# Gated scan and top-1 mixture of experts: the first 192 steps go through both frequent experts in place of being sorted by expert

## The chip, the cores and the metric

The kernel runs on one core of a Trainium2 chip. The metric is the device time of one execution in microseconds (us). An engine takes its instructions in the order in which the program lists them; the engines are PE (TensorE, matrix products), DVE (VectorE), ACT (ScalarE), POOL (GpSimd) and SP (SyncE, which here only starts transfers). They wait for each other by semaphores.

## The reference, cut to what matters

Four sequences of 5056 steps and 256 channels run through a gated linear recurrence. Each of the 20224 resulting tokens then goes to one of eight experts, a two-layer network, and is multiplied by the probability of that expert.

```python
batch, seq, d_model = (4, 5056, 256)
N, D, E, F = (20224, 256, 8, 1024)
...
for t in range(S):
    h = a_t[:, t] * h + x_gated[:, t]
    y[:, t] = h
...
logits = x @ w_gate + modality_bias[modality_id]
e_idx = np.argmax(logits, axis=1)
...
for e in range(E):
    mask = e_idx == e
    h = np.maximum(x[mask] @ w1[e], 0.0)
    out[mask] = gate_w[mask, None] * (h @ w2[e])
```

There are two modalities, and the bias of each (spread 0.5) is large against the rest of the logits. The reference's own router on its default inputs gives 10051 tokens to expert 4, 10124 to expert 7, 49 to expert 2 and none to the others. Of the 768 tokens in the first 192 steps of the four sequences it gives 389 to expert 4, 377 to expert 7 and 2 to expert 2.

## The kernel before, in words

**Chunks.** The sequences are cut along time into the chunks of `CHUNKS` (first step, steps): two of 128 steps, eighteen of 256, one of 128 and one of 64. A chunk holds four times as many tokens as steps. For each chunk ACT and DVE compute the gates and run the scan (`scan_chunk`; on DVE the wide operations on tiles `g` and `x`, and the scan over `a`, `g`), scale and split the result into two fp16 halves in place of `a` (`split_chunk`; `mxy`, `miy`, `scy` and `ivy` belong to its scale), PE computes the logits into `psl`, and DVE finds each token's expert, its place among that expert's tokens, and its gate (`route_chunk`; `l`, `ky`, `oh`, `cu`, `dt`, `be`, `di`, `sg`). `be` counts, for each expert, the rows given out so far. `rows_part` transposes the tokens (SP, tile `rt`) and POOL scatters each as a row to its expert's stretch of the buffer `rows` in device memory.

**Pages.** The experts work on pages of 256 or 128 rows that are read back from `rows` (SP: tile `X` transposed, and `mt` with the token's number and gate). The `HOT` = 2 experts of largest bias, here 4 and 7, have their weights converted to fp16 halves once, in `hw`; `wr` holds them as they come from memory, in four buffers. `choose_two` takes one page for each of the two experts (here called a round): `u` is how far an expert's pages have got, `sel` the rows at which the two pages begin, which SP reads. While the program is built, `choose_pages` adds rounds as long as the tokens of the chunks routed so far, less a margin (`behind`), cover them. The numbers of rounds and pages are thus fixed in the program, while which rows a page holds is decided on the chip. Before the change that gives one round of 128 rows, 38 rounds of 256, then a last round of 256 and one of 128, whose pages take what is left of their expert; and one page of 128 (`choose_cold`) for the expert with most tokens outside the two, whose weights are loaded and converted for it (`cold_weights`, raw tiles `cr`, converted `cw`).

**Layers.** A page's first layer (`ph`, 48 products) is followed by ACT and DVE, which write its result as two fp16 halves `H`; the second layer (`po`) follows, ACT multiplies by the gate (`ot`), and POOL scatters the 128 rows to the output. The first layer of a page is interleaved with the second layer of the page before it.

**What is left over.** When the fixed pages are through, the program compares what has been given out with what the pages took (`over`, `left_over`). If a row is left, `more_pages` runs two more pages of 128, each with the weights of its expert loaded and converted anew, then looks again, and so on. Each engine has a branch of its own there (L1157).

**Order.** The instructions of all engines are written out by a planner that runs while the program is built: the generators ask for an engine and an assumed duration, and of those that could begin at about the same time the one of lowest priority number goes next. `START` gives the order of the first loads: chunk 0, the first expert's two matrices, chunk 1, the second expert's, chunk 2. `HI` says which engine writes the upper fp16 halves of each weight matrix (A is ACT, D is DVE).

Of the kernel before, what the change touches and what calls it, by code (L numbers as in the profile page):

```python
# [9 lines left out]
F32 = mybir.dt.float32  # L10
# [23 lines left out]
HOT = 2  # L34
WAIT = 3.0
WINDOW = 0.1
PART = 8
BACKLOG = 9000
LOOK = 384
HI = "ADADAD"  # L40
LO = "DDDDDD"
START = "0 w w 1 w w 2"
W_AT = 9
C_STEP = 2
URGENT = 0.1
ROW_STEP = 2.4
LAG = 3.0
W_STEP = 0.1

# [6 lines left out]
def columns(c):  # L56

    return B * CHUNKS[c][1] // P


# [14 lines left out]
def kernel(  # L75
# [80 lines left out]

    u = const.tile([1, HOT], F32, name="u")
    nc.vector.tensor_scalar(out=u, in0=key[:, 0:HOT, 0], scalar1=NCAP / 256.0, scalar2=None, op0=ALU.mult)
    cold = const.tile([1, E], F32, name="cold")
    nc.vector.tensor_scalar(out=cold, in0=ev, scalar1=HOT - 0.5, scalar2=8.0, op0=ALU.is_ge, op1=ALU.mult)  # L160
# [269 lines left out]
    def load_chunk(c):  # L430

        t0, T = CHUNKS[c]
        cols = 2 * B * T
        base = 2 * B * t0
        z = T / 256
        got = []
        if f"{c}" in loads:
            yield "SP", 0.0, seen(("turn", loads.index(f"{c}") - 1)), 0.0
        else:
            yield "SP", 0.0, allof(drained(sum(B * t for _, t in CHUNKS[: c + 1]) - BACKLOG), seen(("load", c - 1))), -3.0  # L440
        for i, (name, src) in enumerate((("a", rs), ("g", gs), ("x", xs))):
            tag = "H" if c == 0 and name != "g" else name
            yield "DMA", 2.9 * z, room(tag), -9.0
            tickets[c, name] = tag, take(tag)
            t = (pm if tag == "H" else pa).tile([P, cols], F32, name=f"{name}{c}", tag=tag, bufs=BUFS[tag])
# [95 lines left out]
    wg16 = const.tile([P, 2, 2 * E], F16, name="wg16")  # L541
    ivg = const.tile([P, 1, 1], F32, name="ivg")

    def gate_weights():
# [6 lines left out]
        ps = psl.tile([P, 512], F32, name="psg", tag="lg")  # L551
        yield from power_of_two("g", mx[:, 0:1], 1, ps, sc[:, 0:1], ivg)
        give("lg", tl)
        yield "DVE", 0.07, None
# [21 lines left out]
    def split_chunk(c):  # L576
# [4 lines left out]
        z = T / 256  # L581
        lag = LAG if c > 6 else 0.2
        yield "DVE", 0.07 + 2.13 * z, allof(seen(("scan", c)), room("lg"), seen("gate"), *([seen(("sized", c - 1))] if c else [])), lag
# [36 lines left out]
        for k in range(C):  # L620
            if k % 2 == 0:
                yield "PE", 0.2, None, 1.25 if c > 6 else 0.0
            mm = [(s, h) for s in range(2) for h in range(2)]
# [6 lines left out]
        y_free(c)  # L630

    def y_free(c):
        if ("lg", c) in mark and all(("tr", c, j) in mark for j in range(parts(c))):
            done(c, "a")

    def rows_part(c, j):
# [17 lines left out]
        y_free(c)  # L654

        if T < P:
            for u in range(2):
                nc.gpsimd.iota(
                    rt[64 * u : 64 * u + 64, 0:k, D], pattern=[[2 * S, k]], base=t0 + S * u, channel_multiplier=1
                )  # L660
        else:
            nw = T // P
            nc.gpsimd.iota(
                rt[:, 0:k, D].rearrange("p (q w) -> p q w", w=nw), pattern=[[S, k // nw], [P, nw]],
                base=t0 + S * (PART * j // nw), channel_multiplier=1,
            )
        yield "DVE", 0.07, seen(("route", c)), 0.0
# [4 lines left out]
        for u in range(k):  # L672
            yield "POOL", ROW_STEP if c > 6 else 1.3, None
            scatter(f"rows{c}", rt[:, u, 0:ROW], di[:, PART * j + u : PART * j + u + 1])
# [3 lines left out]
    def route_chunk(c):  # L678
        C = columns(c)
        order = [("route", c - 1)] if c else []  # L680
        lag = LAG if c > 6 else 0.2
        yield "DVE", 0.2, seen(("lg", c), *order)
# [28 lines left out]
        oh = sm.tile([P, E, C], F16, name=f"oh{c}", tag="oh")  # L711
        nc.vector.tensor_tensor(out=oh, in0=ky, in1=mx.broadcast_to(sh), op=ALU.is_equal)
        yield "DVE", 0.13, None
        cu = sm.tile([P, E, C], F16, name=f"cu{c}", tag="cu")
# [40 lines left out]
        di = sm.tile([P, C], I32, name=f"di{c}", tag="di", bufs=6)  # L755
        nc.vector.tensor_copy(di, df)
        tiles["route", c] = di, sg
# [4 lines left out]
    def scatter(group, src, idx):  # L762
# [12 lines left out]
        if "pe" in count:  # L775
# [3 lines left out]
            )  # L779

    nt = const.tile([P, ROW], I32, name="nt")
# [3 lines left out]
    nc.gpsimd.tensor_copy(nf, pidx.broadcast_to([P, E]))  # L785

    def null_rows():
# [18 lines left out]
    class Page:  # L806
        pass

    pages, queue = [], []
    count = {"chosen": 0, "ended": False, "cold": 0, "rows": 0}  # L810
# [9 lines left out]
    def enough():  # L820
# [17 lines left out]
    def queue_page(pg):  # L838
        pg.n = len(pages)
        pages.append(pg)  # L840
        if pg.n == 0:
            add(load_rows(), (1, 2), plan["end"])
            add(expert_layers(), (5, 0), plan["end"])

# [126 lines left out]

    class Tile:
        pass

    def load_rows(n=0):
        while True:
# [5 lines left out]
            if True:  # L982
# [4 lines left out]
                t = Tile()  # L987
                t.tx = take("X")
                t.pg, t.n = pg, f"{pg.n}"
# [21 lines left out]
    def layer1_tail(t, f2, ph, tp):  # L1011
# [11 lines left out]
        mark["h", t.n, f2] = plan["end"]  # L1023

    def layer2_tail(t, a, po, tp):
# [4 lines left out]
        free["DMA"] = max(free["DMA"], plan["end"] - 1.04) + 0.37  # L1030
        ins = nc.gpsimd.indirect_dma_start(  # L1031
            out=out[:, :], out_offset=bass.IndirectOffsetOnAxis(ap=t.mt[:, a, 0:1], axis=0),
            in_=t.ot[:, a, :], in_offset=None, bounds_check=N - 1, oob_is_err=False,
        ).ins
        tc.declare_no_dep(ins, group="outs", reason="every token has an output row of its own")
        tc.add_to_no_dep_group("outs", ins)
        if a == t.pg.st // P - 1:
            give("ot", t.to)

    def ready_at(t):  # L1040
        return max(t.ready, mark.get(("cw", t.pg.c), FAR) if t.pg.e is None else mark.get(("w", 2 * t.pg.e), FAR))

    def expert_layers():

        prev = None
        while True:
# [7 lines left out]
            for g in range(4):  # L1054
                if cur is not None:
# [5 lines left out]
                    if g == 0:  # L1061
                        cur.th = take("H")
                        used.append((plan["end"], st + (used[-1][1] if used else 0)))
                        cur.H = pm.tile([P, 2, NF, st], F16, name=f"H{cur.n}", tag="H")
# [13 lines left out]
                    if g == 3:  # L1078
                        if cur.tx is not None:
                            give("X", cur.tx)  # L1080
                        if pg.e is None:
                            give("wr", pg.tw[0])
                if prev is not None:
# [9 lines left out]
                    if g == 0:  # L1093
                        conds.append(room("ot"))
                        if pg.e is not None:
                            conds.append(seen(("hot", pg.e)))
                    yield "PE", 1.312 * z, allof(*conds), 0.0
                    if g == 0:
                        prev.to = take("ot")
                        prev.ot = pm.tile([P, na, D], F32, name=f"ot{prev.n}", tag="ot", bufs=3)  # L1100
                        gates = prev.mt[:, :, 1].bitcast(F32)
                        prev.gt = sm.tile([P, na], F32, name=f"gt{prev.n}", tag="gt", bufs=3)
# [18 lines left out]
                    if f == NF - 1:  # L1121
                        add(layer2_tail(prev, a, po, prev.tp), (0, 1), plan["end"] + 0.2)
                    if g == 3:
# [4 lines left out]

    def start_chunk(c):
        add(load_chunk(c), (0, 10 + C_STEP * c))  # L1130
        add(scan_chunk(c), (0, 11 + C_STEP * c), urgent=c == 0)
        add(split_chunk(c), (0, 10 + C_STEP * c), urgent=c == 0)
        add(route_chunk(c), (0, 9 + C_STEP * c), urgent=c == 0)
        for j in range(parts(c)):
# [5 lines left out]
    for m in range(2 * HOT):  # L1140
        add(hot_weights(m), (2, W_AT + W_STEP * m))
    add(choose_pages(), (0, 4), urgent=True)
# [75 lines left out]
```

## Time and profile before

| | us |
|---|---|
| median of 3 runs (lowest, highest) | 986.11 (985.5, 986.31) |
| the profiled execution, by the device | 987.44 |
| its span, first to last instruction | 985.6 |
| PE busy in the span | 894.6 |
| DVE, ACT, POOL busy | 667.6, 568.4, 471.3 |

The profile has a page of totals, and answers to queries of its trace. A row of the timeline gives the start in us, the duration, the engine, the line of the kernel, the operation, what it writes and reads with partitions x elements, how many instructions the row merges, and in brackets how long the engine had been idle and who ended that. A row of groups gives a line's instructions of one shape with their count, then busy us and mean ns of one. A window's row gives for each engine the busy us and the number of instructions, then the granted clock of TensorE (PEclk, 1.00 is full), the share of the transfer engines and GB/s.

### The profile page before, as it was taken

Reading aid. Unit: us, or ns where it says so; the run is one execution under the profiler, and the core shown is the slowest. Engines: PE = TensorE matmul, PEld = TensorE weight load, DVE = VectorE, ACT = ScalarE, POOL = GpSimd, SP = SyncE. Lnnn points to the kernel's source line nnn. Section 1 sums busy time; section 2 is a strip of 40 time slices with the busy share of each in tenths; the row PEclk is TensorE's granted clock in tenths of the full one; section 3 lists DMA queues with packets and bytes.
Section 4 is the critical chain, followed back from the end, with each engine's and each line's share of the span. In section 5 each row is a group of like instructions: output and inputs, shape, how many; then the busy total and the mean of one; then the engine's idle time right before and its main releaser. Section 6 shows DMA issues by size and latency. Waiting matters only on the chain. (4 is left out here: it accounts for less than half of the span.)

```text
span 985.6 us, 22594 instructions
## 1 busy us (share of the span) xinstructions
PE 894.6 (91%) x8700; PEld 791.9 (80%) x8700; DVE 667.6 (68%) x1531; ACT 568.4 (58%) x790; POOL 471.3 (48%) x501
## 2 busy tenths in 40 slices
PE   2224899999999999999999999999999999999997
PEld 1223787888888888888888888888898988888886
DVE  4989888888998879997788998952353332232321
ACT  6757776878875687758588787533333333333332
POOL 4034655746386673876746675554253111111111
PEclk9997999999999999999999999999999999999999
DMA  8548997877879897699897887554452222222210
GB/s 296 212 144 219 233 215 233 271 156 188 225 161 232 220 251 222 130 208 197 267 247 171 202 176 171 130 116 102 118 130 71 57 50 53 51 50 55 50 39 19
DMA packets 221176, 156.13 MB, mean 158 GB/s; under 512 B 197953, under 2 KB 201154, under 8 KB 214146
## 3 DMA queue, kind: packets, MB, share of 16 engines
q1 hardware_dynamic: 204178, 110.43, 47.6%
q0 software_dynamic: 16176, 43.98, 13.7%
q8 instruction: 70, 1.15, 0.5%
q14 instruction: 48, 0.39, 0.1%
q10 hardware_dynamic: 704, 0.18, 0.1%
HBM read 68.76 MB, written 44.35 MB: 115 GB/s over the span
## 5 line engine op out<-in xcount | busy, mean ns | idle before, releaser
L1075 PE MATMUL ph<-X,hw 128*128 128x256 f16 (+1 forms) x3936 | 476.4, 272 | 2.6 <-DMA X<-rows 2.6
L1117 PE MATMUL po<-hw,H 128*128 128x256 f16 x3840 | 473.1, 273 | 5.9 <-DVE H L1018 5.9
L1117 PEld LDWEIGHTS <-H 128*128 128x128 f16 x3864 | 372.9, 98 | 51.9 <-DVE H L1018 6.7
L1075 PEld LDWEIGHTS <-hw 128*128 128x128 f16 x3936 | 376.7, 99 | 46.9 <-issue 3.0
L1018 DVE SCALAR_TENSOR_TENSOR H<-ph,H 128x512 f16<-128x512 f32 (+1 forms) x332 | 219.9, 669 | 250.5 <-ACT H L1016 247.1
L1031 POOL DMA_INDIRECT out_dram<-ot,mt x161 | 205.9, 1279 | 297.9 <-ACT ot L1027 239.2
L1016 ACT ACTIVATE H<-ph 128x512 f16<-128x512 f32 (+1 forms) x332 | 191.5, 580 | 269.0 <-PE ph L1075 264.6
L763 POOL DMA_INDIRECT rows<-rt,di x158 | 206.4, 1306 | 184.8 <-PE ph L1075 55.6
L1027 ACT ACTIVATE ot<-po,gt 128x256 f32<-128x256 f32 x161 | 76.0, 472 | 87.7 <-PE po L1117 66.5
L497 DVE TENSOR_TENSOR_SCAN g<-a,g 128x2048 f32<-128x2048 f32 (+2 forms) x22 | 87.8, 3990 | 0.8
L607 ACT ACTIVATE a<-g,scy 128x512 f16<-128x512 f32 (+2 forms) x88 | 54.9, 670 | 7.1 <-DVE miy L520 4.9
L610 DVE SCALAR_TENSOR_TENSOR a<-g,scy,a 128x512 f16<-128x512 f32 (+2 forms) x88 | 56.9, 693 | 0.0
L483 DVE TENSOR_TENSOR g<-g,x 128x2048 f32<-128x2048 f32 (+2 forms) x22 | 45.5, 2069 | 8.6 <-ACT x L481 8.5
L474 ACT ACTIVATE a<-a,ch 128x1024 f32<-128x1024 f32 (+2 forms) x44 | 49.4, 1146 | 0.1
L477 ACT ACTIVATE x<-a 128x2048 f32<-128x2048 f32 (+2 forms) x22 | 38.1, 1733 | 17.2 <-issue 10.5
L469 DVE SCALAR_TENSOR_TENSOR g<-g,x 128x2048 f32<-128x2048 f32 (+2 forms) x22 | 45.6, 2075 | 0.4 <-ACT g L465 0.4
L586 DVE TENSOR_REDUCE mxy<-g 128x4 bf16<-128x2048 f32 (+2 forms) x22 | 45.3, 2059 | 0.2 <-issue 0.2
L625 PEld LDWEIGHTS <-a 128*128 128x128 f16 x632 | 25.5, 97 | 19.7 <-ACT a L607 10.8
L481 ACT ACTIVATE x<-x 128x2048 f32<-128x2048 f32 (+2 forms) x22 | 38.2, 1736 | 4.4 <-DVE x L479 4.2
L465 ACT ACTIVATE g<-g 128x2048 f32<-128x2048 f32 (+2 forms) x22 | 38.1, 1734 | 2.8 <-DMA g<-in_i_gate_dram 2.7
L467 ACT ACTIVATE a<-a 128x2048 f32<-128x2048 f32 (+2 forms) x22 | 38.0, 1726 | 0.0
L625 PE MATMUL psl<-wg,a 128*128 128x16 f16 x632 | 26.6, 170 | 12.1 <-DVE a L610 5.9
(174 smaller groups left out, 438.4 us busy)
## 6 DMA issues: line engine op xcount, KB each, us to landing
a<-in_r_gate_dram SPq DMA_DIRECT2D x18, 1024.0 KB
g<-in_i_gate_dram SPq DMA_DIRECT2D x18, 1024.0 KB
x<-in_x_dram SPq DMA_DIRECT2D x18, 1024.0 KB
wr<-in_moe_w_dram SPq DMA_DIRECT2D x4, 1024.0 KB
out_dram<-ot,mt POOLq DMA_INDIRECT x161
rows<-rt,di POOLq DMA_INDIRECT x158
cr<-in_moe_w_dram SPq DMA_DIRECT2D x2, 1024.0 KB
a<-in_r_gate_dram SPq DMA_DIRECT2D x3, 512.0 KB
```

The lines of the kernel that those rows point to most:

```text
L474: nc.scalar.activation(sl, sl, AF.Exp, scale=ch[:, h : h + 1], bias=ch[:, h : h + 1])
L497: nc.vector.tensor_tensor_scan(out=g, data0=a, data1=g, initial=0.0, op0=ALU.mult, op1=ALU.add)
L607: nc.scalar.activation(ys[:, 0, :, g, :], yg[:, :, g, :], AF.Copy, scale=sc[:, g : g + 1])
L610: nc.vector.scalar_tensor_tensor(out=ys[:, 1, :, g, :], in0=yg[:, :, g, :], scalar=sc[:, g : g + 1], in1=ys[:, 0, :, g, :], op0=ALU.mult, ...
L625: nc.tensor.matmul(ps[:, 2 * E * k : 2 * E * (k + 1)], yc[:, s, h, k, :], wg16[:, h, :], start=(m == 0), stop=(m == len(mm) - 1),)
L763: ins = nc.gpsimd.indirect_dma_start(out=rows[:, :], out_offset=bass.IndirectOffsetOnAxis(ap=idx, axis=0), in_=src, in_offset=None, bounds ...
L1016: nc.scalar.activation(t.H[:, 0, hs, :], ph[:, :, 0:st], AF.Relu)
L1018: nc.vector.scalar_tensor_tensor(out=t.H[:, 1, hs, :], in0=ph[:, :, 0:st], scalar=0.0, in1=t.H[:, 0, hs, :], op0=ALU.max, op1=ALU.subtract,)
L1027: nc.scalar.activation(t.ot[:, a, :], po, AF.Copy, scale=t.gt[:, a : a + 1])
L1031: ins = nc.gpsimd.indirect_dma_start(out=out[:, :], out_offset=bass.IndirectOffsetOnAxis(ap=t.mt[:, a, 0:1], axis=0), in_=t.ot[:, a, :], i ...
L1075: ins = nc.tensor.matmul(ph[:, v, 0:st], lhsT, rhs, start=(m == 0), stop=(m == len(mm) - 1))
L1117: ins = nc.tensor.matmul(po, lhsT, rhs, start=(f == 0 and m == 0), stop=(f == NF - 1 and m == len(mm) - 1))
```

## The change: what it does

The first two chunks of 128 steps become three of 64 and one of 128, and the chunks of 256 begin at step 320 and end the cut with one of 128 (`CHUNKS`). The chunks 0, 1 and 2, of 64 steps and 256 tokens each, are `DENSE`. Their tokens do not go through pages if they belong to one of the two frequent experts: PE applies each of the two experts to all 256 tokens as they lie in `a`, six tiles in the order of `DENSE_ORDER` (chunk, part, expert). `dense_tail` multiplies a tile's result by the token's gate if the token belongs to that expert and by 0 if not (`g2`, `gt`); ACT writes the first expert's part to `do`, DVE adds the second's, and POOL scatters the sum to the output. `route_chunk` makes for these chunks three rows of masks (`h3c`, `sel3`: first expert, second, any other), counts in `be` only the tokens of other experts, and gives the rest a row number outside `rows`, which the scatter skips.

In `enough` and `choose_pages` the tokens of the dense chunks now count as none (`rows_of`). The rounds in the program become one of 128, then 36 of 256, then the last one of 256 and the last of 128; 79 pages in place of 83, besides the six dense tiles. All upper halves of the two experts' weights are now written by ACT (`HI`), the weights' conversion goes ahead of the chunks (`W_AT`), and expert work is started by the dense tiles (`expert_layers` is added at the start and no longer by the first page).

```diff
-CHUNKS = [(0, 128), (128, 128)] + [(256 + 256 * k, 256) for k in range(18)] + [(4864, 128), (4992, 64)]
+CHUNKS = [(0, 64), (64, 64), (128, 64), (192, 128)] + [(320 + 256 * k, 256) for k in range(18)] + [(4928, 128)]
+DENSE = 3
-HI = "ADADAD"
+HI = "AAAAAD"
-W_AT = 9
+W_AT = [2, 2, 4, 4]
+DENSE_ORDER = [(0, 0, 0), (1, 0, 0), (0, 0, 1), (1, 0, 1), (2, 0, 0), (2, 0, 1)]
+def rows_of(c):
+    return B * CHUNKS[c][1] if c >= DENSE else 0
...
+    def dense_ready(t):
+        at = allof(seen(*[("split", t.c, j) for j in range(parts(t.c))], ("w", 2 * t.pg.e)))()
+        if at < FAR and t.c not in dense:
+            ys = tiles[t.c][0].bitcast(F16).rearrange("p (x n) -> p x n", x=4)
+            o = pm.tile([P, columns(t.c), D], F32, name=f"do{t.c}", tag=f"do{t.c}", bufs=1)
+            dense[t.c] = ys, o
+        return at
...
@@ route_chunk
+        if c < DENSE:
+            nc.vector.tensor_tensor(
+                out=h3c, in0=oh.rearrange("p (o e) c -> p o e c", o=1).broadcast_to(s4), in1=hot3.broadcast_to(s4), op=ALU.mult
+            )
+            nc.vector.tensor_reduce(out=sel3, in_=h3c.rearrange("p r e c -> p r c e"), axis=AX.X, op=ALU.add)
+            oh = h3c[:, HOT]
...
+            nc.vector.scalar_tensor_tensor(
+                out=df, in0=sel3[:, HOT], scalar=-float(NULL_ID), in1=df, op0=ALU.mult, op1=ALU.add
+            )
+            nc.vector.tensor_scalar(out=di, in0=df, scalar1=float(NULL_ID), scalar2=None, op0=ALU.add)
+            nc.vector.tensor_tensor(out=gd[:, 0], in0=tiles["iv", c][0], in1=sg, op=ALU.mult)
+            nc.vector.tensor_tensor(out=g2, in0=sel3[:, 0:HOT], in1=gd.broadcast_to([P, HOT, C]), op=ALU.mult)
+            nc.vector.scalar_tensor_tensor(
+                out=to, in0=sel3[:, HOT], scalar=float(NULL_ID), in1=tokens[c], op0=ALU.mult, op1=ALU.add
+            )
...
@@ enough, choose_pages
-            have += B * CHUNKS[c][1]
+            have += rows_of(c)
-            have = sum(B * t for _, t in CHUNKS[: routed(plan["end"])])
+            have = sum(rows_of(c) for c in range(routed(plan["end"])))
...
+    def dense_tail(t, a, po, tp):
+        _, o = dense[t.c]
+        k = 2 * t.i + a
+        if a == 0:
+            nc.vector.tensor_scalar(out=t.gt, in0=gates, scalar1=hiv[t.pg.e], scalar2=None, op0=ALU.mult)
+        if t.pg.e == 0:
+            nc.scalar.activation(o[:, k, :], po, AF.Copy, scale=t.gt[:, a : a + 1])
+            return
+        nc.vector.scalar_tensor_tensor(
+            out=o[:, k, :], in0=po, scalar=t.gt[:, a : a + 1], in1=o[:, k, :], op0=ALU.mult, op1=ALU.add
+        )
+        put_out(o[:, k, :], tiles["gates", t.c][1][:, k : k + 1])
...
+    for c, i, e in DENSE_ORDER:
+        dense_tile(c, i, e)
+    add(expert_layers(), (5, 0))
```

On DVE, before the change, the first pages are chosen (L863 to L875) behind the scan of the third chunk (L497); `psl_550` holds the second chunk's logits:

```order
L497 SCALAR_TENSOR_TENSOR g_433<-a_406,g_433 128x2048
L863 TENSOR_TENSOR d_644<-b_575,u 1x2
L685 TENSOR_REDUCE l_646<-psl_550 128x32
L865 TENSOR_SCALAR d_644<-d_644 1x2
L867 SCALAR_TENSOR_TENSOR sel_643<-u,d_644 1x2
L873 TENSOR_SCALAR d_644<-d_644 1x2
L875 TENSOR_TENSOR u<-u,d_644 1x2
```

Nothing of an expert's layers stands ahead of this choice. After the change DVE has, behind the scan of the fourth chunk, the tails of the dense tiles: `Hd` is the lower half of a dense tile's hidden layer, `do` the sum of the two experts, `g_640<-g_640,x_858` the first wide operation of the fifth chunk.

```order
L1102 SCALAR_TENSOR_TENSOR Hd_0_1_1040<-phd_0_1_0_1041,Hd_0_1_1040 128x512
L721 TENSOR_TENSOR l_1108<-l_1108,ivl_989 128x16
L482 SCALAR_TENSOR_TENSOR g_640<-g_640,x_858 128x2048
L1102 SCALAR_TENSOR_TENSOR Hd_0_1_1040<-phd_0_1_1_1095,Hd_0_1_1040 128x512
L1117 TENSOR_SCALAR gtd_0_1_1168<-g_833,hiv_219 128x2
L1124 SCALAR_TENSOR_TENSOR do_507<-pod_0_1_0_1066,gtd_0_1_1168,do_507 128x256
```

Such tails of the six dense tiles (24 of `Hd`, 6 of `do` by DVE) are new between the chunks' own work.

The first pages are now chosen further down on DVE, behind the routing of the fifth chunk (`di_1760`) and the first wide operation of the sixth:

```order
L794 TENSOR_REDUCE df_1758<-dt_1748 128x8
L818 CAST di_1760<-df_1758 128x8
L482 SCALAR_TENSOR_TENSOR g_1602<-g_1602,x_1667 128x2048
L950 TENSOR_TENSOR d_1767<-b_1643,u 1x2
L700 TENSOR_TENSOR rt_0_1717<-ivy_1506,sg_1742 128x8
L952 TENSOR_SCALAR d_1767<-d_1767 1x2
L954 SCALAR_TENSOR_TENSOR sel_1766<-u,d_1767 1x2
```

The choice has thus moved behind the work of further chunks and behind all dense tiles.

At the end of the fixed pages DVE stands before the change as follows; the branch is L1157, and the rows behind it are those of `more_pages`:

```order
L1103 TENSOR_SCALAR gt_14986<-mt_14632,hiv_216 128x1
L1018 SCALAR_TENSOR_TENSOR H_14893<-ph_3_14964,H_14893 128x256
L1157 TENSOR_LOAD over_14410
L1157 COMPARE_AND_BRANCH
L890 TENSOR_TENSOR k_15038<-be,tk 1x8
L904 SCALAR_TENSOR_TENSOR k_15038<-k_15038,tieb 1x8
```

After the change the same rows stand there under new line numbers, behind four pages fewer. On SP, which starts the transfers, the rows behind its branch (L1281 after the change) are these, `X_15388` being the first further page and `cr_0` the first of its expert's two weight matrices (`ISA` rows set registers):

```order
L1281 COMPARE_AND_BRANCH
L1069 TENSOR_LOAD sel_15347
L1069 ISA x2
L1080 ISA
L1080 DMA_TRANSPOSE X_15388<-rows 128x4x128
L1081 ISA
L1081 DMA mt_15389<-rows 128x2
L410 TENSOR_LOAD sel_15347
L410 ISA x2
L378 ISA
L378 DMA cr_0_15401<-in_moe_w_dram 128x2x1024
```

Nothing moved on this stretch but its place: it stands behind 79 pages where it stood behind 83. What a row of these lists does not tell is how long it takes or waits.

More of the change, by code (lines that the diff above doesn't have):

```diff
@@ L542 @@
     ivg = const.tile([P, 1, 1], F32, name="ivg")
+    hot3 = const.tile([P, HOT + 1, E, 1], F16, name="hot3")
     def gate_weights():
@@ L630, in split_chunk, with dense_tile @@
         y_free(c)
+    def dense_tile(c, i, e):
+        t = Tile()
+        t.pg = Page()
+        t.pg.st, t.pg.e, t.c, t.i, t.tx, t.n = 256, e, c, i, None, f"d{c}_{i}_{e}"
+        queue.append(t)
+    def dense_ready(t):
[5 more added lines that the diff above has]
+        return at
+    dense = {}
     def y_free(c):
-        if ("lg", c) in mark and all(("tr", c, j) in mark for j in range(parts(c))):
+        taken = all(("taken", *t) in mark for t in DENSE_ORDER if t[0] == c)
+        if taken and ("lg", c) in mark and all(("tr", c, j) in mark for j in range(parts(c))):
             done(c, "a")
@@ L654, in rows_part @@
         y_free(c)
[L656 to L666, printed above, removed]
+        numbers(rt[:, :, D], c, j)
         yield "DVE", 0.07, seen(("route", c)), 0.0
@@ L785 @@
     nc.gpsimd.tensor_copy(nf, pidx.broadcast_to([P, E]))
+    tokens = {}
+    for c in range(DENSE):
+        ti = const.tile([P, columns(c)], I32, name=f"ti{c}")
+        numbers(ti, c, 0)
+        tokens[c] = const.tile([P, columns(c)], F32, name=f"tn{c}")
+        nc.gpsimd.tensor_copy(tokens[c], ti)
     def null_rows():
@@ L807 @@
         pass
+    class Tile:
+        pass
     pages, queue = [], []
@@ L1023, in layer1_tail, with put_out @@
         mark["h", t.n, f2] = plan["end"]
+    def dense_tail(t, a, po, tp):
+        _, o = dense[t.c]
+        k = 2 * t.i + a
+        yield "DVE", 0.07, allof(seen(("gates", t.c)), seen(("hot", t.pg.e))), 0.0
+        if a == 0:
+            t.gt = sm.tile([P, 2], F32, name=f"gt{t.n}", tag="gt", bufs=3)
+            gates = tiles["gates", t.c][0][:, t.pg.e, k : k + 2]
+            nc.vector.tensor_scalar(out=t.gt, in0=gates, scalar1=hiv[t.pg.e], scalar2=None, op0=ALU.mult)
+        if t.pg.e == 0:
+            yield "ACT", 0.36, None
+            nc.scalar.activation(o[:, k, :], po, AF.Copy, scale=t.gt[:, a : a + 1])
+            give("po", tp)
+            return
+        yield "DVE", 0.36, None
+        nc.vector.scalar_tensor_tensor(
+            out=o[:, k, :], in0=po, scalar=t.gt[:, a : a + 1], in1=o[:, k, :], op0=ALU.mult, op1=ALU.add
+        )
+        give("po", tp)
+        yield "POOL", 1.04, None
+        put_out(o[:, k, :], tiles["gates", t.c][1][:, k : k + 1])
+    def put_out(src, idx):
+        free["DMA"] = max(free["DMA"], plan["end"] - 1.04) + 0.37
+        ins = nc.gpsimd.indirect_dma_start(
+            out=out[:, :], out_offset=bass.IndirectOffsetOnAxis(ap=idx, axis=0),
+            in_=src, in_offset=None, bounds_check=N - 1, oob_is_err=False,
+        ).ins
+        tc.declare_no_dep(ins, group="outs", reason="every token has an output row of its own")
+        tc.add_to_no_dep_group("outs", ins)
     def layer2_tail(t, a, po, tp):
@@ L1029, in layer2_tail @@
         yield "POOL", 1.04, None
[L1030 to L1036, printed above, removed]
+        put_out(t.ot[:, a, :], t.mt[:, a, 0:1])
         if a == t.pg.st // P - 1:
```

96 lines of the change are left out of this document (73 added, 23 removed).

## The prediction

> **What bounds the kernel now.** I read the windows first, then TensorE's timeline and waits at both ends, then DVE's groups, then the transfers of the last pages.
>
> ```profile
> 0.00:100.00 100.00, 31.24 (x309) 26.46 (x310) 80.80 (x205) 66.52 (x71) 33.27 (x105) 0.93 0.69 220
> 100.00:600.00 500.00, 485.45 (x4794) 427.02 (x4793) 434.57 (x913) 365.50 (x471) 319.03 (x272) 0.99 0.83 209
> 600.00:978.00 378.00, 377.70 (x3606) 338.46 (x3602) 152.22 (x415) 135.91 (x248) 118.03 (x124) 1.00 0.33 78
> ```
>
> The columns behind the length are PE, weight loads, DVE, ACT, POOL. From 100 us on PE is busy 485.45 of 500 and 377.70 of 378 us: the number of pages sets the time. In the first 100 us it idles 68.8 us while DVE is busy 80.8.
>
> ```profile
> PE psl L507 <- DVE mxy L586: 32.7, 9, 12.1
> ```
>
> ```profile
> 69.29 5.28 PE L1075 MATMUL ph<-X,hw 128*128 128x128 f16 x48 [1.31 <-DMA X<-rows]
> 96.05 0.27 PE L507 MATMUL psl<-identb,mxy 128*4 128x128 bf16 x1 [12.13 <-DVE mxy L586]
> 97.85 2.72 PE L1075 MATMUL ph<-X,hw 128*128 128x256 f16 x12 [1.30 <-DMA X<-rows]
> 925.54 1.47 PE L1075 MATMUL ph<-X,hw 128*128 128x256 f16 x12
> 926.85 1.47 PE L1117 MATMUL po<-hw,H 128*128 128x256 f16 x12
> 974.79 3.44 PE L1117 MATMUL po<-hw,H 128*128 128x256 f16 x30
> ```
>
> PE waits for DVE's frontend (32.7 us in all). Two small pages run from 69.29; the stream of full pages begins at 97.85 and its last product ends at 974.79 + 3.44 = 978.2. Twelve products take 926.85 - 925.54 = 1.31 us, a page of 256 rows has 96, so 10.48 us.
>
> Which pages hold what can be read from the bytes that the last output scatters moved; first the stretch 963.1 to 967.1, then that from 979.0 to the end:
>
> ```profile
> q0 software_dynamic: 48, 0.07, 5.2%
> ...
> q0 software_dynamic: 48, 0.01, 1.1%
> ```
>
> A token's output is 1 KB. The pages fixed before the change hold 128 + 38 x 256 + 256 + 128 = 10240 rows for each frequent expert. Expert 4 has 10051 tokens, so its last page of 256 begins at 9856 and holds 195, its second half 67: 0.07 MB. Expert 7 has 10124, its last page begins at 10112 and holds 12: 0.01 MB. The data on the chip are thus the reference's default inputs, and every token fits, by 116 rows.
>
> **The change, part by part.**
>
> *Fewer pages.* Four full pages go: 4 x 10.48 = -41.9 us from a stretch where PE never waits. Six dense tiles of the same 96 products come, 62.9 us of PE, but in the first 100 us and a little after, where PE stood idle.
>
> *The frontend gets longer.* Dense tiles put work on DVE, the busiest engine there.
>
> ```profile
> L1018 DVE SCALAR_TENSOR_TENSOR H<-ph,H 128x512 f16<-128x512 f32 x312 | 211.5, 685 | 234.1 <-ACT H L1016 230.7 <-ACT a L467 1.4 <-issue 1.3
> L497 DVE TENSOR_TENSOR_SCAN g<-a,g 128x2048 f32<-128x2048 f32 x18 | 79.7, 4427 | 0.6
> L610 DVE SCALAR_TENSOR_TENSOR a<-g,scy,a 128x512 f16<-128x512 f32 x72 | 50.8, 747 | 0.0
> L469 DVE SCALAR_TENSOR_TENSOR g<-g,x 128x2048 f32<-128x2048 f32 x18 | 41.3, 2296 | 0.0
> L483 DVE TENSOR_TENSOR g<-g,x 128x2048 f32<-128x2048 f32 x18 | 41.2, 2287 | 7.8 <-ACT x L481 7.8
> L586 DVE TENSOR_REDUCE mxy<-g 128x4 bf16<-128x2048 f32 x18 | 41.0, 2277 | 0.0
> L479 DVE TENSOR_SCALAR x<-x 128x2048 f32<-128x2048 f32 x18 | 22.5, 1248 | 3.2 <-ACT x L477 3.1
> L1018 DVE SCALAR_TENSOR_TENSOR H<-ph,H 128x256 f16<-128x256 f32 x20 | 8.4, 423 | 16.4 <-ACT H L1016 16.4
> ```
>
> Neighbours on DVE overlap by some 0.07 us, so I count each duration less that. Up to the choice of the first pages of 256 rows: 24 lower halves `H`, 24 x 0.61 = 14.6 us; six additions into `do`, which no row shows, priced as the 128x256 row, 6 x 0.35 = 2.1 (it also reads `do`; ACT's half of the work is hidden, as ACT was idle 33 of the first 100 us); three routings with 8 more small operations of about 0.12, 3; gates 0.8. Five chunks are routed by then (576 steps) in place of three (512): 64 steps more are a quarter of 2.3 + 1.25 + 2.29 + 4.43 + 2.28 + 4 x 0.75 = 15.5, so 3.9, and two more chunks' small operations (some 30 of 0.12) 7.5. Off go two upper halves of weights, now ACT's (4 x 0.75 = -3.0), and four tails of the second small page (-1.4). Sum +28 to +31 us of DVE. To this come waits between three busy engines, bounded below by -2 (the first loads are smaller) and above by +14, twice DVE's idle time from 50 to 100 us (5.3) and something for ACT; I take +3. The full pages then start at 97.85 + 33 = 131, and the fixed pages end at 978.2 + 33 - 41.9 = 969, **-9 us** (between -20 and +6). SP's transposes for three small chunks and POOL's six scatters of rare tokens lie beside this; if that cover went, the rare page is wanted only after all chunks and nothing would wait.
>
> *The pages no longer hold the tokens.* After the change the fixed pages hold 128 + 36 x 256 + 256 + 128 = 9728 rows an expert. Outside the dense chunks expert 4 has 10051 - 389 = 9662 tokens, expert 7 has 10124 - 377 = 9747: **19 too many**. The planner took 1024 rows of pages away for 766 tokens that go elsewhere. So the branch is entered: two more pages of 128 with weights loaded and converted anew, behind everything. Before, this did not happen: one cold page only, of 48 products, is in the trace, and `cr` was loaded twice, for two matrices.
>
> ```profile
> L1075 PE MATMUL ph<-X,cw x48: 218/219/220, 768.3 to 774.8; 128*128 128x128 f16 x48
> ...
> L366 SPq DMA_DIRECT2D cr<-in_moe_w_dram x2: 372/378/383, 706.0 to 709.8; - x2
> L329 ACT ACTIVATE cw<-cr,csc x2: 1135/1142/1148, 720.6 to 722.2; 128x1024 f16<-128x1024 f32 x2
> L332 DVE TENSOR_SCALAR cw<-cr,csc x2: 745/745/745, 729.6 to 732.2; 128x1024 f16<-128x1024 f32 x2
> L335 DVE SCALAR_TENSOR_TENSOR cw<-cr,csc,cw x4: 1277/1284/1285, 721.8 to 733.0; 128x1024 f16<-128x1024 f32 x4
> ```
>
> The steps of such a page, all in the trace:
>
> ```profile
> 8.33 1.61 SPq L366 DMA_DIRECT2D wr<-in_moe_w_dram x2
> 13.41 1.89 PE L301 MATMUL pt<-wr 128*128 128x128 bf16 x16 [5.23 <-DMA wr<-in_moe_w_dram]
> 15.34 0.29 DVE L304 SCALAR_TENSOR_TENSOR jk<-pt,ident 128x128 f32<-128x128 f32 x1 [4.50 <-PE pt L301]
> 16.70 0.15 DVE L288 TENSOR_SCALAR iv<-sc 128x1 int32<-128x1 int32 x1
> 703.42 0.14 DVE L890 TENSOR_TENSOR k<-be,tk 1x8 f32<-1x8 f32 x1
> 704.91 0.30 DVE L921 CAST sel<-sf 1x2 int32<-1x2 f32 x1
> 950.63 1.22 SPq L996 DMA_TRANSPOSE X<-rows  x1
> 952.16 0.35 SPq L997 DMA_DIRECT2D mt<-rows  x1
> 975.40 0.43 DVE L1018 SCALAR_TENSOR_TENSOR H<-ph,H 128x256 f16<-128x256 f32 x1 [0.78 <-ACT H L1016]
> ```
>
> Counted from the last fixed product, M: DVE passes its branch at M - 2.2 (its last `H` ends at 975.8); choice 705.21 - 703.42 = 1.8; SP reads `sel`, starts the page's transfers (952.51 - 950.63 = 1.9), then the weights, as far from the choice as 706.0 from 705.2: M + 2.6. They land after 13.41 - 8.33 = 5.1: 7.7. Scale, 16.85 - 13.41 = 3.4: 11.1. First matrix, 1.14 + 2 x 1.28 = 3.7: 14.8. Second matrix, landed meanwhile, the rest of its scale 1.5 and 2 x (0.745 + 1.28) = 4.05: 20.4; the first layer's 48 products lie under this. The halves `H` on DVE 1.9, second layer behind the last of them 978.2 - 975.8 = 2.4: **M + 24.7**. The second page's weights need buffers of `wr`, all four in use; the first is free at 14.8, so they land at 20.7, under the first page. From 24.7 on: 3.4 + 3.7 + 1.5 + 4.05 + 1.9 + 2.4 = 17: **M + 41.7**. Then the end as before. Bounds: 34, if transfers land sooner in idle queues and steps overlap; 56, if PE works at half rate and the branches cost what PE's did when it jumped, 3.4 us each.
>
> ```profile
> L1157 PEldq COMPARE_BRANCH  x1: 3408/3408/3408, 976.7 to 976.7; - x1
> ```
>
> For the rate there is one row, after 13 us in which PE had 0.5 us of work (PEclk is the column 0.50):
>
> ```profile
> 97.00:100.00 3.00, 2.15 (x11) 1.49 (x11) 2.90 (x12) 1.54 (x1) 0.00 (x0) 0.50 0.94 260
> ```
>
> The 12 products at 97.85 took 2.72 us, 227 ns each, where 109 is the rule later. The added pages leave PE idle for some 8 us at a time, so I take half of the slow price for two second layers (24 products, 2.6 or 5.2 us) and round: **+44**. The Trainium skill ("TensorE: Matmul & The Clock Gate", "What's actually happening") says that TensorE's clock is halved after about 3.4 us of idling and comes back only after about as long at work, with which this row agrees; by that rule all of the second layers and scales of these pages would run at half rate, and the extra work would cost 48.
>
> *The sum*: -9 + 44 = +35. Against the profiled execution's span 985.6 that is 1020.6. The execution took 987.44 by the device, the median is 986.11; I put the sum on the median: **1021 us**.
>
> **The rivals.** *(1) PE never waits once the dense tiles begin.* For it: PE has room, 68.8 us. Then full pages would begin when 62.9 us of tiles and 12 of small pages are done, from about 36 us, at 113: +15 - 41.9 + 44 gives 1003. Against it: DVE's sum alone leads to 126 or more. *(2) The chains of dense tile, ACT and DVE, each in order, hold the chunks up far more* than DVE's sum: full pages from about 150, +52 - 42 + 44, 1040. ACT's and DVE's lists alternate chunk and tile work, but four `ph` buffers part them. *(3) Faster: no row is left over.* The branch (L1157, now L1281) is the one place that decides: at 9728 tokens or fewer for expert 7 its price is 0 and -9 remains, 977; with one more it is the whole 44, as whole pages with their weights are taken. For it speaks only that 19 is few; against it, that the counts, checked above by 67 and 12 rows to the token, leave no room, and that a skipped round would leave more rows over, never fewer.
>
> **How the numbers follow.** The forecast, overflow with a start set by DVE, 0.80; rival 1 0.08; rival 2 0.08; rival 3 0.04. The range takes the bounds of the overflow (34 to 56) and of the start (-20 to +6), not all at their worst together: 1000 to 1044. A difference within 0.2% (2 us) is about what a measurement of this kernel cannot tell from none; slower by more has 0.95, faster 0.04, the same 0.01.
>
> **What would show it.** Right: six tiles of 96 products between about 35 and 110 us; full pages from about 131; four `cr` loads more than before; PE's last fixed product near 969, then some 42 us in which PE is mostly idle, waiting for weights and for DVE's conversions. Wrong: only two `cr` loads, which makes rival 3; full pages before 118 or after 145; or a tail beyond 56 us.

## The result: slower by 4.2%, and the profile after

| | before | after |
|---|---|---|
| median, us (lowest, highest) | 986.16 (985.5, 986.31) | 1028.29 (1026.13, 1029.77) |
| profiled execution by the device; its span | 987.44; 985.6 | 1027.39; 1025.5 |
| last product of the fixed pages ends, M | 978.23 | 980.60 |
| last product of all ends | that one | 1018.19 |

The ratio is 1.0424 (95% interval 1.0412 to 1.0437). The spans differ by 39.9 us: the fixed pages end 2.4 us later, where I had forecast 9 earlier, and 37.6 us of work follow them, where I had forecast 44.

**The front.** PE's timeline after, at the last dense tile, the first small page, the first full pages and the end of the fixed pages:

```profile
100.81 2.78 PE L1237 MATMUL pod<-hw,Hd 128*128 128x256 f16 x24
...
117.07 5.30 PE L1189 MATMUL ph<-X,hw 128*128 128x128 f16 x48 [7.82 <-DMA X<-rows]
...
135.15 2.74 PE L1189 MATMUL ph<-X,hw 128*128 128x256 f16 x12 [3.70 <-DMA X<-rows]
...
977.16 3.44 PE L1237 MATMUL po<-hw,H 128*128 128x256 f16 x30
```

The full pages begin at 135.15 in place of 97.85. The dense tiles fill the time in which PE idled before, and end at 100.81 + 2.78 = 103.59. The window from the first dense products to the last (columns: PE, weight loads, DVE, ACT, POOL, clock, transfer share, GB/s):

```profile
30.00:104.00 74.00, 69.03 (x644) 58.85 (x642) 68.68 (x213) 53.75 (x78) 18.56 (x22) 1.00 0.36 112
```

Two engines are nearly full there: PE 69.03 and DVE 68.68 of 74 us. DVE's new work costs within half a microsecond what I priced, by the groups of the first 136 us:

```profile
L1102 DVE SCALAR_TENSOR_TENSOR Hd<-phd,Hd 128x512 f16<-128x512 f32 x24 | 16.0, 682 | 1.3 <-ACT Hd L1100 1.2
L1124 DVE SCALAR_TENSOR_TENSOR do<-pod,gtd,do 128x256 f32<-128x256 f32 x6 | 2.9, 481 | 1.6 <-PE pod L1237 1.5
```

Behind the last dense tile comes a chain. The fifth chunk is routed, POOL scatters its eight columns, and only then may SP load pages of 256 rows. The first and the third row are POOL's last two scatters of that chunk, between them stands DVE's choice, and the last row is SP's load. SP's waits from 128 to 137 us follow:

```profile
124.28 4.60 POOL L825 DMA_INDIRECT rows<-rt,di  x1 [0.30 <-issue]
128.36 0.15 DVE L954 SCALAR_TENSOR_TENSOR sel<-u,d 1x2 int32<-1x2 f32 x1
129.19 0.98 POOL L825 DMA_INDIRECT rows<-rt,di  x1 [0.31 <-issue]
...
131.93 1.26 SPq L1080 DMA_TRANSPOSE X<-rows  x1
```

```profile
SPq L1069 <- DVE sel L954: 7.8, 1, 7.8
SPq L1080 <- DMA rows<-rt,di: 2.7, 1, 2.7
```

SP waits for the choice, and then 2.7 us more for the last scatter to land. Before the change the load followed the choice at once, 0.9 us later:

```profile
93.26 0.15 DVE L867 SCALAR_TENSOR_TENSOR sel<-u,d 1x2 int32<-1x2 f32 x1
...
94.20 1.27 SPq L996 DMA_TRANSPOSE X<-rows  x1
```

**The fixed pages.** In the window 200 to 300 PE is busy 97.44 us before and 92.10 after; PE's wait for DVE's `mxy`, between 135 and 960 us, has doubled (in us: total, times, longest). Before, then after:

```profile
PE psl L507 <- DVE mxy L586: 5.9, 6, 1.7
```

```profile
PE psl L520 <- DVE mxy L607: 12.0, 8, 3.4
```

**The end.** `cr` is loaded six times where it was loaded twice, and PE's timeline from M on shows two pages one after the other:

```profile
cr<-in_moe_w_dram SPq DMA_DIRECT2D x6, 1024.0 KB
```

```profile
988.63 1.89 PE L313 MATMUL ptc<-cr 128*128 128x128 bf16 x16 [8.03 <-DMA cr<-in_moe_w_dram]
992.25 1.89 PE L313 MATMUL ptc<-cr 128*128 128x128 bf16 x16 [0.76 <-DMA cr<-in_moe_w_dram]
1000.65 0.38 PE L1237 MATMUL po<-cw,H 128*128 128x256 f16 x2
1001.43 2.58 PE L1237 MATMUL po<-cw,H 128*128 128x256 f16 x22 [0.40 <-DVE H L1102]
1003.84 1.08 PE L313 MATMUL ptc<-cr 128*128 128x128 bf16 x16
...
1015.61 2.58 PE L1237 MATMUL po<-cw,H 128*128 128x256 f16 x22 [0.65 <-DVE H L1102]
```

The first page's last product ends at 1004.01 = M + 23.4, the second's at 1018.19, 14.2 later.

### The profile page after: what moved, and what is told of

It is laid out like the page before. It is cut to its first block, busy times and chain, and to the rows that moved or that the text cites. A ratio compares the mean times of both kernels' runs of the same rounds, so it can differ in the third digit from the quotient of the medians.

```text
span 1025.5 us, 23649 instructions
## 1 busy us (share of the span) xinstructions
PE 942.5 (92%) x9114; PEld 832.5 (81%) x9114; DVE 700.1 (68%) x1665; ACT 589.1 (57%) x827; POOL 484.2 (47%) x516
## 5 line engine op out<-in xcount | busy, mean ns | idle before, releaser
L1189 PE MATMUL ph<-X,hw 128*128 128x256 f16 (+1 forms) x3744 | 454.8, 273 | 13.5 <-DMA X<-rows 13.5
L1237 PE MATMUL po<-hw,H 128*128 128x256 f16 x3648 | 449.4, 273 | 1.6 <-DVE H L1102 1.6
L1189 PEld LDWEIGHTS <-hw 128*128 128x128 f16 x4032 | 388.1, 99 | 62.1 <-DMA X<-rows 14.0
L1237 PEld LDWEIGHTS <-H 128*128 128x128 f16 x3720 | 359.1, 98 | 46.2 <-DVE H L1102 3.9
L1102 DVE SCALAR_TENSOR_TENSOR H<-ph,H 128x512 f16<-128x512 f32 (+1 forms) x324 | 211.5, 662 | 232.7 <-ACT H L1100 232.1
L1133 POOL DMA_INDIRECT out_dram<-ot,mt x155 | 196.5, 1268 | 315.2 <-ACT ot L1142 257.7
L1100 ACT ACTIVATE H<-ph 128x512 f16<-128x512 f32 (+1 forms) x324 | 184.9, 575 | 275.4 <-PE ph L1189 274.1
L825 POOL DMA_INDIRECT rows<-rt,di x158 | 219.7, 1390 | 153.1 <-PE ph L1189 40.4
L1189 PE MATMUL phd<-a,hw 128*128 128x256 f16 x288 | 36.9, 283 | 1.4 <-DVE a L631 1.4
L1237 PE MATMUL pod<-hw,Hd 128*128 128x256 f16 x288 | 34.8, 273 | 1.8 <-ACT do L1120 1.7
```

The source lines that it names most:

```text
L825: ins = nc.gpsimd.indirect_dma_start(out=rows[:, :], out_offset=bass.IndirectOffsetOnAxis(ap=idx, axis=0), in_=src, in_offset=None, bounds ...
L1100: nc.scalar.activation(t.H[:, 0, hs, :], ph[:, :, 0:st], AF.Relu)
L1102: nc.vector.scalar_tensor_tensor(out=t.H[:, 1, hs, :], in0=ph[:, :, 0:st], scalar=0.0, in1=t.H[:, 0, hs, :], op0=ALU.max, op1=ALU.subtract,)
L1133: ins = nc.gpsimd.indirect_dma_start(out=out[:, :], out_offset=bass.IndirectOffsetOnAxis(ap=idx, axis=0), in_=src, in_offset=None, bounds_ ...
L1189: ins = nc.tensor.matmul(ph[:, v, 0:st], lhsT, rhs, start=(m == 0), stop=(m == len(mm) - 1))
L1237: ins = nc.tensor.matmul(po, lhsT, rhs, start=(f == 0 and m == 0), stop=(f == NF - 1 and m == len(mm) - 1))
```

## The experiments

The experiments ran on three chips, and these differ: the kernel before took 985.09 us on the first, which ran the four kernels below up to the dense tiles without their lower halves, 1005.14 on the second and 1004.70 on the third. (In the result's own comparison it took 986.16.) So each kernel is compared with the kernel before on its own chip. M is read from each kernel's own profile, which is that of one execution.

**One round more.** The change, with a second last round of 128 rows:

```diff
-        for size in (256, P):
+        for size in (256, P, P):
```

> The changed kernel with one more last round of 128 rows (two pages), so that the 19 rows left over have a place and the branch isn't entered. Theory (the two pages behind the branch cost the loss, 1018.2 - 980.6 = 37.6 us in the profile of the changed kernel): 37.6 us go, two pages of 128 at 5.3 us come, 1028.3 - 37.6 + 10.6 = 1001 us. Rival (the dense tiles and their frontend cost the loss, and rows have to be worked on in any place): 1028 to 1039 us.

1000.78 us, ratio 1.0144 (1.0115 to 1.0173), two `cr` loads, M at 987.42 + 3.44 = 990.86. The round costs 10.3 us, and all that came behind M is gone. The work behind M was the 19 rows left over; 128 rows more for each expert remove it. The kernel is still slower than the one before by 1.4%, some 14 us, of which the round is 10.3.

**The kernel before with a round less**, 12 rows of expert 7 left over:

```diff
-        for size in (256, P):
+        for size in (256,):
```

> The kernel before with its last round of 128 rows left out: its pages then hold 10112 rows an expert, 12 too few for the 10124 tokens of expert 7, and the branch is entered without any dense tile. Theory: two pages of 128 go (10.6 us), the branch's two pages come (37.6 us), 986.2 + 27 = 1013 us. Rival (dense tiles cost the loss): 976 to 981 us, a little work less.

1009.49 us, ratio 1.0236 (1.0209 to 1.0262), with six `cr` loads:

```profile
cr<-in_moe_w_dram SPq DMA_DIRECT2D x6, 1024.0 KB
```

M is at 965.0 and the last product ends at 999.8, so the branch costs 34.7 us in a kernel that has no dense tile at all. The price belongs to the branch. (The time is 3.5 us below what I expected; 2.9 of it is this price against 37.6.)

**One further page instead of two:**

```diff
-    more_pages(2, (N + E * (P - 1)) // P)
+    more_pages(1, (N + E * (P - 1)) // P)
```

> The changed kernel with one page in place of two at the first look behind the branch; 19 rows need one. Theory (the second page comes wholly after the first, from 1004.0 to 1018.2 us in the profile of the changed kernel): 14.2 us go, 1014 us. Rival (the two pages overlap, or the branch's own cost and code loading make the price): 1023 to 1028 us.

1013.56 us, ratio 1.0275 (1.0248 to 1.0303); the last product ends at M + 23.1. Against the ratio of the change that is 14.7 us less, close to the 14.2 that the trace of the change shows between the two pages. The second page is taken for no rows (only expert 7 has any left), and hides behind nothing.

**The dense tiles without their lower halves**, so that DVE has 24 operations of 682 ns less before the first full page; PE does as many products as in the change, with the upper half in the place of the lower.

```diff
+        if t.c is None:
             nc.vector.scalar_tensor_tensor(
                 out=t.H[:, 1, hs, :], in0=ph[:, :, 0:st], scalar=0.0, in1=t.H[:, 0, hs, :],
...
-                            (prev.H[:, hx, f, rs_], wv[:, wx, f])
+                            (prev.H[:, hx if prev.c is None else 0, f, rs_], wv[:, wx, f])
```

> The changed kernel without the lower fp16 halves of the dense tiles' hidden layers on DVE (24 operations of 0.61 us, 14.6 us); PE makes the same number of products and reads the upper half in their place, so the sum lacks the low term there. The rows left over stay. Theory (DVE's list sets when full pages begin): full pages begin 10 to 15 us earlier than at 135.2, 1028.3 - 12 = 1016 us. Rival A (PE's dense tiles set it): 1028 us. Rival B (POOL's scatters of the chunks' rows set it, of which the last ended 2 us after the choice): full pages earlier by 5 us or less, 1023 us or more.

1022.93 us, ratio 1.0363 (1.0334 to 1.0392). Of 14.6 us taken from DVE, only 1.5 come back at the first full page (133.65) and 3.3 at M (977.33). Two other kernels with the front of the change, the one with a round more and the one with a single further page, ran on the same chip and began their full pages at 136.66 and 136.22; against these it is 3. The same window, then DVE's longest wait in it:

```profile
30.00:104.00 74.00, 70.21 (x667) 59.97 (x667) 58.37 (x195) 54.85 (x80) 20.64 (x24) 1.00 0.44 119
```

```profile
DVE do L1125 <- PE pod L1238: 6.5, 4, 2.6
```

DVE has 10 us less to do and now waits for PE's dense products instead. That DVE alone sets the start is wrong. The time itself is what rival B gave (POOL's scatters), and part of that is in the trace: the choice came at 125.35, 3.0 earlier than in the change, and 1.5 of this went into the scatters and the load behind it (8.3 us from the choice to the full pages, 6.8 in the change).

**The same, and without the third product of the dense second layers** (96 products fewer, 10.5 us of PE):

```diff
-                            for hx, wx in ((0, 0), (0, 1), (1, 0))
+                            for hx, wx in (((0, 0), (0, 1), (1, 0)) if prev.c is None else ((0, 0), (0, 1)))
```

> As the run without the dense tiles' lower halves (1022.9 us), and in their second layers the third product of each three is left out too: 6 tiles x 16 x 0.109 = 10.5 us less of PE's work, none of DVE's, so the low term is missing and its stand-in as well. Theory (with DVE relieved, PE's dense stream sets the pace: 70.2 of 74 us busy between 30 and 104): full pages begin 7 to 10 us earlier, 1014 us. Rival (the waits of chunk work on ACT, SP and POOL set it): 1021 us or more.

1022.73 us, ratio 1.018 (1.0148 to 1.0213) on the second chip, where the 1014 and the 1021 that I had worked out from times of the first chip decide nothing. The full pages begin at 125.55, 8.1 earlier than without the lower halves alone on the first chip. As the second chip had not run the change, I ran both kernels on the third:

> The changed kernel itself, beside the next three on one chip, since chips differ (the kernel before took 985.09 us on one and 1005.14 on another). Theory: the ratio to the kernel before on the same chip is again about 1.042, and its trace shows what of the difference between chips lies in which part of the program. Rival: what costs time on the other chip is not shared by both kernels, and the ratio is off by more than 0.006.

> The dense tiles without lower halves of their hidden layer and without the third product of their second layers (that part of the arithmetic is left out), beside the changed kernel on one chip. Theory, that the dense tiles' stream on TensorE sets where the full pages begin, together with DVE: full pages begin 9 to 10 us earlier than in the changed kernel, the fixed pages end as much earlier, and the time is 1.030 to 1.033 times the kernel before. Rival, that the start of the full pages is not what sets the end: the time stays within 4 us of the changed kernel's on this chip.

The change there: 1031.65 us, ratio 1.0259 (1.0231 to 1.0287). The reduced kernel: 1025.52, ratio 1.0218 (1.0189 to 1.0247). The first full pages, in the change and then in the reduced kernel:

```profile
139.16 2.74 PE L1189 MATMUL ph<-X,hw 128*128 128x256 f16 x12 [4.59 <-DMA X<-rows]
```

```profile
126.05 2.74 PE L1190 MATMUL ph<-X,hw 128*128 128x256 f16 x12 [5.13 <-DMA X<-rows]
```

The start moves by 13.1 us, where four traces of the change's own front lie between 135.15 and 139.16, so PE's dense stream has a part in it. In the change, its repeat and the three traces of reduced kernels the choice of the full pages comes 24.0 to 25.6 us behind the last dense product, with the lower halves and without. Which part is PE's alone is not shown: no kernel leaves out the third products and keeps the lower halves. M comes at 973.07 in place of 988.39, so in these two traces the whole gain at the start reaches the end. But they show the slowest of four executions of the change and the fastest of four of the reduced kernel. The medians differ by 6.1 us only, and the two intervals overlap a little: the time lies between what I expected and the rival's bound, and how much of the start reaches the median is not settled. The expectation for the change itself failed: its ratio is not 1.042 everywhere. On this chip the kernel before loses 19 us and the change 3. The kernel before was not profiled there, so where it loses them stays open.

**Fewer dense chunks.** The new cut with no dense chunk, with two, and with one and a round more:

```diff
-DENSE = 3
+DENSE = 0    # DENSE_ORDER = []
+DENSE = 2    # DENSE_ORDER: the first four tiles
+DENSE = 1    # DENSE_ORDER: the two tiles of chunk 0; for size in (256, P, P)
```

> The changed kernel with no dense chunk: the new cut of the chunks, the weights' order and ACT's upper halves remain, and every token goes through pages, 83 as before. Theory (dense tiles delay full pages and buy two rounds): full pages begin at 95 to 100 us as before, 986 us (982 to 992). Rival (the cut into small chunks itself delays the frontend, by the 30 small operations of each further chunk): 993 us or more.

> The changed kernel with two dense chunks in place of three: four dense tiles, one round of 256 more, and no row is left over. Against the changed kernel 37.6 us of the branch go and 21 us of pages come. Theory now (the stream of dense tiles on PE sets when full pages begin): they begin up to 17 us earlier, 995 us. Rival (DVE's list sets it, in which the choice of the first pages of 256 stands 7 us of work further down than with three dense chunks): 1015 us or more.

> One dense chunk (two tiles) and one more last round of 128 rows: 38 rounds of 256 and three of 128, no row left over, which is 10.5 us of pages less than before the change. Theory: the dense tiles end at about 53 us, under the frontend's work on the next chunks, full pages begin at 102 to 110 us, 982 to 990 us. Rival (already the first dense tiles cost as much start as they save): 992 us or more.

On the second chip: 1001.53 us (ratio 0.9971, 0.995 to 0.9991), 1000.93 (0.9962, 0.9945 to 0.998) and 997.48 (0.9923, 0.9907 to 0.994). None has rows left over (two `cr` loads each). In microseconds all are above what was expected, on a chip where the kernel before is 20 us above it too; by ratio the cut alone is nearly neutral, and two dense chunks lie below both what I expected (995 would be 1.009) and the rival's 1015. The reason that I gave for two chunks failed, though: their full pages begin no earlier than the change's.

```profile
139.70 4.81 PE L1189 MATMUL ph<-X,hw 128*128 128x256 f16 x24 [6.63 <-DMA X<-rows]
```

From 30 to 104 us PE is busy 50.85 of 74 us in that kernel and DVE 69.65: PE is no longer full, and DVE's list sets the start, as the rival had it: the choice, at 132.88, stands behind the split of the sixth chunk, where the change has it right behind that chunk's scan. The time is good all the same. The two pages more (21 us of PE) lengthen the stretch from there to M by only 8.3 us against the trace of the change (853.7 and 845.4): PE idles 10.5 us in it in place of 17.9, and the second layer of the second small page falls ahead of it. The kernel with one dense chunk ran again on the third chip, and so did a version with wider chunks behind the dense one:

> One dense chunk of 64 steps instead of three, and one round of 128 more, so that no token is left over. Theory: as before, 0.990 to 0.994 times the kernel before; full pages begin within some 5 us of where they began before the change, and one round of 128 fewer (10.5 us of TensorE) is what remains. Rival: the earlier ratio of 0.992 was that chip's, and here the two are the same within 0.3%.

> As the one before, but the chunks behind the dense one are wider at once: 64, 128, then 256 steps. Theory (each chunk costs DVE some 4 us of small operations whatever its length, and one chunk fewer stands ahead of the full pages): up to 4 us below the kernel with one dense chunk and chunks of 64, 64, 64, 128. Rival (a wider chunk holds the first full pages back, as they wait for its whole scan): 3 to 8 us above it.

```diff
-CHUNKS = [(0, 64), (64, 64), (128, 64), (192, 128)] + [(320 + 256 * k, 256) for k in range(18)] + [(4928, 128)]
+CHUNKS = [(0, 64), (64, 128), (192, 256)] + [(448 + 256 * k, 256) for k in range(18)]
```

One dense chunk: 1002.07 us, ratio 0.9967 (0.9947 to 0.9988), full pages from 101.89. It is faster again, but the gain of 0.3% is about what the rival named, not my 0.6 to 1%. The early start is not the whole story, as PE stands still once more behind it:

```profile
144.44 2.74 PE L1189 MATMUL ph<-X,hw 128*128 128x256 f16 x12 [11.80 <-DMA X<-rows]
```

Wider chunks: 1018.62, ratio 1.0144 (1.0121 to 1.0166), full pages from 131.86: the rival, and worse than its 3 to 8 us. In the wide version PE waits 6.9 us at once for the `mxy` of a 256-step chunk ahead of them:

```profile
PE psl L520 <- DVE mxy L607: 8.0, 2, 6.9
```

Whether one dense chunk gains on a chip where the kernel before takes 985 us was not measured.

## Why the prediction was right, and what was off

The time lies in the range, the direction is right, and the branch that I named is most of the loss. The closeness of 1028 to 1021 is in part luck: the fixed pages came out 11.4 us worse than forecast and the branch 6.4 better.

*The pages no longer hold the tokens*: shown. Six `cr` loads; one round more removes all of it, one round less brings it into the kernel before. In my sum the 19 rows decided the sign; in the measurement they decided the size, as the fixed pages alone end 2.4 us later than before. The price was mis-sized: 37.6 in place of 44. Up to the last conversion of the first page's weights, at M + 20.4, the steps held, with the landing 5.25 after the issue (forecast 5.1). Three terms were too large. From the last conversion to the last product (halves `H` and second layer) each page took 3.05 us where I had 4.3, so the first page was done at M + 23.4 (forecast 24.7). The second page took 14.2 where I had 17: besides that, its first scale took 2.25 us, not 3.4, with 16 products in 1.08 us and not the 1.89 of the cold row that I used. And the 2.3 us that I added for second layers at half rate were not spent: their 22 products took 2.58 us, 117 ns each. The clock (the last column but two) shows why, in windows of the first scale, the first layer and the second layer:

```profile
988.00:991.00 3.00, 1.98 (x17) 1.72 (x17) 0.30 (x2) 0.00 (x0) 0.00 (x0) 0.50 1.15 311
...
996.00:1000.00 4.00, 4.00 (x39) 4.00 (x40) 3.40 (x7) 0.77 (x2) 0.00 (x0) 0.52 0.70 249
1000.00:1004.20 4.20, 3.80 (x46) 3.28 (x44) 2.48 (x7) 0.88 (x3) 0.00 (x0) 1.00 0.55 172
```

After 8 us of idling PE works at 0.50; the 48 first-layer products keep it busy for some 3.5 us at that rate, under DVE's conversion, and when the second layer comes the clock is at 1.00. I had counted the slow start of PE and forgotten that the first layer of the same 128 rows is the work that ends it. The Trainium skill ("TensorE: Matmul & The Clock Gate", "What's actually happening") gives full rate after some 3.4 us of sustained work, with which these windows agree.

*Fewer pages, -41.9*: from the first full page to M the span shrank by 880.4 - 845.4 = 34.9, so 7.0 less than that. 2.6 of these are the second layer of the second small page, which ended ahead of the full pages before and stands among them now. 3.1 more are waits of PE (17.9 us idle in place of 14.9): DVE, with the same chunk work but behind by 37 us, makes PE wait 12.0 us for `mxy` in place of 5.9, and other waits became fewer. The rest is of the size of one more stretch at a low clock: behind waits of 2.0 and 3.4 us the granted clock is 0.75 from 189.69 to 196.60 and 0.67 from 206.90 to 212, where the kernel before has one such stretch behind its first full pages, 0.69 from 122.58 to 128. My estimate from these windows is 1.7 us. I had put the cost of all this at nothing.

*The frontend gets longer, +33 at the start of the full pages*: measured 37.3. The choice on DVE came 35.1 later (128.36 against 93.26). Up to it DVE was busy 105.0 us in place of 74.2, 30.8 more, and idle 4.3 more: the size that I gave, 28 to 31 and 3, though the terms that I listed add up to 27.5 only. The other 2.2 are the scatter: choice to full pages took 6.79 us and took 4.59 before, and SP's wait for `rows` is in the trace. I had named POOL's scatters of rare tokens as covered and not looked at those of the chunk that the first pages need.

The cause that I gave for this was half right: "DVE's sum sets the start" failed as the only cause. With 14.6 us less on DVE the start moves by 1.5 to 3 us, as DVE then waits for PE's dense stream, nearly full as well; with PE relieved too it moves by 13. Rival 1 had PE's stream as the bound, yet its 113 left out the chain behind the last tile: from 103.6 on, routing, scatter and load took 31.6 us, in which PE had 11 us of small pages to do. Rival 2 asked for a start at 150 and rival 3 for no row left over; neither came.

*Sum*: +2.4 + 37.6 = +40 where I had -9 + 44 = +35.

## What to carry to other kernels

Where a program's capacity is fixed when it is built and its need is decided by the data, count the need against the capacity before pricing anything else: four pages fewer shortened the full pages' stretch by 35 us, and 19 rows too many cost 37.6. When work is moved under idle time of one engine, add up every engine in that stretch and the chain that follows it; here PE's idle time was free, but DVE was busy 80.8 of the first 100 us already, PE became full, and the start slid by 37 us. That alone used up what the pages saved. Where two engines are full, an experiment that frees one of them can show little: freeing DVE moved the start by 1.5 to 3 us, freeing both by 13.

## What the runs showed of the hardware that I had not expected

The same two kernels differ by 1.0424 (1.0412 to 1.0437) in the first comparison and by 1.0259 (1.0231 to 1.0287) on another chip, with the kernel before at 986.16 and 1004.70 us and the change at 1028.29 and 1031.65. So a difference of a per cent between two versions is known only for the chip on which both ran. The work behind M took 37.6 us in the one trace of the change and 1023.46 + 2.88 - 988.39 = 37.95 in the other, so between these two traces it is the part ahead of M that varies. Why the kernel before loses more on that chip than the change is not shown.
